# A hand-planned attention and MLP kernel: a new PE group order, load order and planner constants

## The chip, the cores and the metric

The kernel runs on one NeuronCore of a Trainium2 chip. Its time is the device time of one execution in microseconds (us); the figure that is compared is the median of several executions. A profile is one execution taken by the hardware profiler, with its own time.

The engines are named as in the profile: PE is TensorE (matmuls), PEld its weight loads, DVE is VectorE, ACT is ScalarE, POOL is GpSimd, SP is SyncE, which here does nothing but issue transfers; "SPq" is SP's queue of issues.

## What is computed

Streaming attention (four sink tokens and a window of 128) over 4 batches, 8 heads, 768 tokens and 64 dimensions, and then an MLP with the activation h * sigmoid(beta * h) on the 3072 x 512 result:

```python
keep = (pos[None, :] < 4) | ((rel >= 0) & (rel < 128))      # rel = query - key
scores = where(keep, q @ k.T / 8, -1e9);  a = softmax(scores);  x = a @ v
...
h = x @ w_in                              # 3072x512 @ 512x2048
g = h * (1.0 / (1.0 + exp(-beta * h)))
out = g @ w_out                           # 3072x2048 @ 2048x512
```

Inputs and outputs are float32; the kernel multiplies in bf16.

## The kernel before

**Tiling.** The 3072 tokens are eight halves of 384 tokens (hb 0 to 7, two to a batch). In each half there are four units, one for each pair of heads, so 32 units (u). Half 0 and half 1 (XB = 2) get their q and k transposed on PE; from half 2 on the transposes of q and k, and of the attention result, are done by the DMA engines.

**Groups.** Work on PE is cut into groups, each with a letter:

- T: q and k of one pair of heads are transposed on PE (L697) and copied to qkT (halves 0 and 1 only).
- C, D: the scores of one unit, in two parts (L783, weights of 64 rows, so that two matmuls stand side by side). Each takes a pair of PSUM banks. ACT takes the exponential (L792); POOL or DVE masks it (L798, L803, L809).
- S: the scores against the sinks (L819), with the exponential in L823. Its weights kS are made from qkT by POOL (L725).
- A: attention times v (L861, and L851 for the far blocks' sinks with vS, which DVE copies from v in L686). DVE divides by the sum (L866, L868) into onorm.
- X: the attention result is transposed on PE into xT (L880; halves 0 and 1). Later halves use a DMA transpose for it (L891).
- h, g, H: one of the 16 blocks of the first MLP product (L910, four matmuls of 384 columns), followed by tanh on ACT (L915) and the gate on DVE (L917). In halves 0 and 1 it is cut into two groups of two matmuls: h needs xT of head pairs 0 and 1, g that of 2 and 3.
- O: a quarter of a 128-token block of the second product (L931, four matmuls of 512 columns). After the fourth quarter the PSUM bank is copied to one of three buffers osb (by L558 on ACT or L563/L564 on DVE) and stored by SP (L940). The last block is cut into 384 and 128 columns.
- b: the transpose of beta (L602).

**What sets the order.** The constant ORDER is a string of 405 letters: PE does its groups in just this order. A planner, `Graph.schedule`, runs when the kernel is built. It keeps a clock for each engine, places PE's groups in the order of the string, and at each step lets each other engine take the ready operation that can start first; among those of the same start, the one with the longest tail of work behind it. Operations with several possible engines (`any_of`: casts, copies out of PSUM, masks) go where their estimated end comes first, with a small penalty for ACT (BIAS). `Graph.place` holds the planner's estimates for transfers: how long an issue takes, how many descriptors fit the ring, when a transfer lands, and what an instruction fetch costs. So the constants in it decide the order of every queue but PE's, and the choice of engines; none of them is executed on the chip. `fillers` puts matmuls on a constant tile (P<-ones, L1027) wherever the planner sees PE wait, up to 48 us by its own clock.

`resolve` then turns the plan into semaphore waits. [...]

**Loads.** All loads are issued by SP in one fixed chain. PAR['l0'] orders the eleven loads of half 0 (indices 0 to 7 are q0, k0, q1, k1, q2, k2, q3, k3, of 192 KB; 8 to 10 are v0, v1, v2, of 256 KB). PAR['mix'] interleaves the loads of half 1 and half 2 ('a') with the 16 weight pieces of 512 KB ('w'; wst and, early on, g's third buffer). Later halves follow in order, each with three blocks of q, of k and of v, in two stage buffers. SP's other work is the DMA transposes of q and k (L734), of onorm (L891) and the stores (L940).

**The lines of the loads and copies.** L635 is every load of q, k and v, L647 every weight load; L558, L560, L563 and L564 are the copies and casts on ACT, POOL and DVE, whatever tile they write.

Of the kernel before, what the change touches and what calls it, by code (L numbers as in the profile page):

```python
# [11 lines left out]
DM, DF, NOUT = 512, 2048, 512  # L12
# [7 lines left out]
EW = 256 * (NB - 1) + 128  # L20


PAR = {'MD': 1, 'XB': 2, 'l0': [0, 2, 6, 1, 3, 4, 9, 5, 7, 10, 8], 'mix': 'aawwaawawawwawwaaaawwawwawwwawaa'}
ORDER = ('TCDTSTTDCSDSCASCTADACbXXAhhhXXThghDghgDhggThgggChhgghgShDSghSghghTghgCASCAXADOXOAhhhhXOXOgOOggOOhghg'
         'hhgOOOghgghghhhghgOgOSDgSChCOghSgADODCCOODOOSAAOAOSSOCCSOSODCHHHHHHHHOHDDOHAHDCHHAHHHAAOODDOOOODCDOH'
         'SCCHHOOASSHHOHOHHHHHSHHHAACSHSOHDCCOAODDOOCCDOAOOHHSHSAOHHOHAAHHHHHHHSHOHOHOSSOCDOHDCCOHHAOOHHHHHSHH'
         'HOSOCCDOHHOHODDAHOAHAOODCCASOOOCDDHHHHHHOAOHOOSHHOOSAHHAOHHHHHOOOHHHHOOHHHHHHOOHHHHOHOOOOOHOOOOOOOOO'
         'OOOOO')


# [6 lines left out]

class Op:
    __slots__ = ("eng", "fn", "deps", "signal", "count", "waits", "sem", "vc", "dma", "seq", "end", "ns", "alts",
                 "group", "tail", "preds", "left", "succ", "at", "queue", "ring", "lag", "x", "tag", "chain")  # L40


class Group:
# [3 lines left out]
class Graph:  # L47
# [1 line left out]
    LAT = {"act": 108, "dve": 85, "gp": 45, "pe": 163, "sp": 0}  # L49
    HOP = {"act": 37, "dve": 33, "gp": 67, "pe": 57, "sp": 26}  # L50
    LAND = {"act": 22, "dve": 23, "gp": 58, "pe": 50, "sp": 26}
    LEAD, PAD, LATE = 1500, 2000, 90000
    BIAS, EARLY = 300, 100000
    FILL_TO = 48000
    RING, FETCH, SWITCH = 165, 900, 85
    DEPTH = 9

    def __init__(self):
        self.ops = []
        self.groups = []  # L60
        self.writers = {}
        self.readers = {}
        self.last_load = None
        self.filler = None

    def begin(self, tag):
# [5 lines left out]
    def add(self, eng, fn, ns=0, r=(), w=(), x=(), dma=None, alts=None, queue=470, ring=64, lag=0, after=(), tag=None):  # L72


        o = Op()
        o.eng, o.fn, o.dma, o.ns, o.alts = eng, fn, dma, ns, alts or {eng: (fn, ns)}
        o.queue, o.ring, o.lag, o.x, o.tag, o.chain = queue, ring, lag, list(x), tag, None
        o.signal, o.count, o.waits, o.vc = False, 0, [], None
        o.group, o.seq = None, -1
        if eng == "pe":  # L80
            o.group = self.groups[-1]
            o.group.ops.append(o)
        deps = []
        for k in r:
            ws = self.writers.get(k)
            assert ws, k
            deps += [(p, True) for p in ws]
        for k in w:
            deps += [(p, False) for p in self.readers.get(k, ())]
            deps += [(p, False) for p in self.writers.get(k, ())]  # L90
        for bs, i in x:
            if eng != "pe":
                deps += [(p, False) for p in bs.users[i] if p.eng == "pe"][-1:]
            bs.users[i].append(o)
            bs.left[i] += 1
        deps += [(p, False) for p in after]
        o.deps = deps
        for k in r:
            self.readers.setdefault(k, []).append(o)
        for k in w:  # L100
            self.writers[k] = [o]
            self.readers[k] = []
        self.ops.append(o)
        return o

    def place(self, o, at):
        o.at = at
        if o.dma:
            self.pending = [x for x in self.pending if x[0] > at]
            issued, need = at + o.queue + 40, min(o.ring, self.RING)  # L110
            total = sum(n for _, n in self.pending)
            for f, n in self.pending:
                if total + need <= self.RING:
                    break
                issued, total = max(issued, f), total - n
            begin = issued + o.lag if o.lag else at + 1150 + o.ns
            self.dma_free = max(self.dma_free + o.ns, begin)
            self.pending.append((self.dma_free, o.ring))
            self.free[o.eng] = issued
            o.end = self.dma_free + 950 + (self.PAD if at > self.LATE else 0)  # L120
        else:
            if o.eng == "pe":
                self.n_pe += 2
                if self.n_pe >= self.fetched + 256:
                    self.fetched += 256
                    self.dma_free = max(self.dma_free, at) + self.FETCH
                rows = o.group is not None and o.group.tag in "CD"
                if rows != self.rows:
                    at = o.at = at + self.SWITCH
                    self.rows = rows  # L130
            self.free[o.eng] = at + o.ns
            o.end = at + o.ns + self.LAT[o.eng]
# [15 lines left out]
    def schedule(self, order):  # L148
# [44 lines left out]
                t = max(t, soft[id(o)].tail + 180)  # L193
            o.tail = t + o.ns + (2000 if o.dma else 0)
        self.free = {e: 800.0 for e in self.ENGINES}
        self.dma_free, self.pending, self.n_pe, self.rows, self.fetched = 0.0, [], 0, False, 0
        new = []
        banks = [(0.0, ())] * 8
        holder = [None] * 8
# [37 lines left out]
        while at_pe < len(todo) or pool:  # L237
# [20 lines left out]
            for o in pool:  # L258
                opts = []
                for e, (fn, ns) in o.alts.items():  # L260
                    t = self.free[e]
                    for p in o.preds:
                        s = self.seen(p, e)
                        if s > t:
                            t = s
                    if o.dma:
                        t = max(t, self.dma_free - self.LEAD)
                    opts.append((t + ns + (self.BIAS if e == "act" and t < self.EARLY else 0), t, e))
                _, t, e = min(opts)
                by_eng.setdefault(e, []).append((t, o))  # L270
# [184 lines left out]
def _program(nc, G, sb, ps, q, k, v, w_in, w_out, beta, out):  # L455
# [274 lines left out]
    def XT(hb, i):  # L730
        n = "qk"[i]
        cs = list(range(NK))
        w = len(cs) * 512
        add("sp", lambda e: e.dma_start_transpose(  # L734
            qkT_all[:, hb % (NT // 4), i, cs[0] * 512:cs[0] * 512 + w].rearrange("p (b t) -> p b t", t=128),
            x16[n][hb % NX][:, cs[0]:cs[0] + len(cs), :, :].rearrange("p c h d -> p (c h d)")), 1500,
            r=[(n + "16", hb % NX, j, c_) for j in range(4) for c_ in cs],
            w=[("qkT", hb % (NT // 4), j, i, c_) for j in range(4) for c_ in cs], dma=f"dx{n}{hb % 2}", queue=1540, ring=999, lag=1350)

# [22 lines left out]
    def SC(u):  # L764
# [23 lines left out]
        for j, grp in enumerate(gs):  # L788
# [5 lines left out]
            for kind_, sg in (("d", 1), ("p", -1)):  # L794
                at_ = [i for i, blk in enumerate(grp) if blk[0] == kind_]
                if at_:
                    d = E[z][:, s0 + at_[0]:s0 + at_[-1] + 1, :, :].rearrange("p s h w -> p (s h) w")
                    alts = {"gp": (lambda e, d=d, sg=sg, at_=at_: e.affine_select(  # L798
                        d, d, [[0, 2 * len(at_)], [sg, 128]], ALU.is_ge, 0.0, base=min(sg, 0), channel_multiplier=-sg),
                        pool_ns(256 * len(at_), 2 * len(at_)))}  # L800
                    mk = maskT[:, kind_ == "p", :].unsqueeze(1).to_broadcast([128, 2 * len(at_), 128])
                    if UNITS[u][0] < PAR.get('MD', 2):
                        alts["dve"] = (lambda e, d=d, mk=mk: e.tensor_tensor(d, d, mk, ALU.mult),  # L803
                                       70 + 256 * len(at_) / 1.9)
                    any_of(alts, r=[("E", z, j), ("maskT", int(kind_ == "p"))], w=[(kind_, z, j)])
            if grp[0][0] == "s":
                d = E[z][:, s0:s0 + 2, :, :]
                mask = maskS[:, :, :].unsqueeze(2).to_broadcast([128, 2, 2, 128])
                fn = lambda e, d=d, mask=mask: e.tensor_tensor(d, d, mask, ALU.mult)  # L809
                any_of({"gp": (fn, 1150), "dve": (fn, 335)}, r=[("E", z, j), "maskS"], w=[("s", z, j)])  # L810

    def SS(u):

# [27 lines left out]
    def AV(u):  # L841
# [5 lines left out]
        for m, ps in enumerate(parts(u)):  # L847
# [8 lines left out]
            for hh in range(2):  # L856
                o0 = (2 * m + hh) * (D + 1)
                for n, (kind_, j, i, kb) in enumerate(ps):
                    vz = (hb if kb >= NK * half else hb - 1) % NV
                    add("pe", lambda e, o0=o0, hh=hh, i=i, kb=kb, vz=vz, a=(n == 0 and not far), o=(n == len(ps) - 1):  # L860
                        e.matmul(A()[:, o0:o0 + D + 1], E[z][:, i, hh, :], vaug[vz][:, kb % NK, 2 * hp + hh, :],  # L861
                                 start=a, stop=o, skip_group_check=True), 39,
                        r=[(kind_, z, j), ("v", vz, kb % NK)], x=[(bs, 0)])
        nb = c1 - c0
        av = lambda: A()[:, 0:2 * nb * (D + 1)].rearrange("p (a e) -> p a e", e=D + 1)
# [22 lines left out]
    def XO(u):  # L888
# [3 lines left out]
            xT[:, hb, hp:hp + 2, :].rearrange("p h (m t) -> p (h m) t", t=128),  # L892
            onorm[:, on:on + 2, :, :].rearrange("p o m d -> p (o m d)")), 700,
            r=[("on", on), ("on", on + 1)], w=[("xT", hp, tl), ("xT", hp + 1, tl)], dma=f"dy{on}", queue=1260,
            ring=60, lag=700)

    hi = [0]

# [26 lines left out]
    def OQ(T_, t, j, a=0, b=NOUT):  # L925
# [9 lines left out]
        if j == 3:  # L935
            z = os_i[0] % NOS
            os_i[0] += 1
            any_of(copies(osb[z][:, a:b], lambda: P[:, bk[0], a:b], {"dve": dve_ns(b - a), "act": act_ns(b - a)}, 0.5), w=[("osb", z)],
                   x=[(bk, 0)])
            add("sp", lambda e: e.dma_start(out_t[NK * hb + t][:, a:b], osb[z][:, a:b]), 640 * (b - a) // NOUT, r=[("osb", z)],  # L940
                dma=f"do{z}", queue=370, ring=8)


# [119 lines left out]
```

The softmax here doesn't subtract the row's maximum and nothing guards it: scores larger than these inputs give would overflow.

## Time and profile before

| | |
|---|---|
| median of 10 runs | 226.74 us (226.16 to 227.82) |
| the profiled execution's own time | 226.32 us |
| its span, first to last instruction | 224.6 us |
| mean granted TensorE clock | 0.992 |
| PE, first and last start of a matmul | 1.06 and 221.49 us |
| DMA traffic | 40.95 MB in 104,741 packets, mean 182 GB/s |
| L910, 512 matmuls | 92.7 us busy |
| L931, 400 matmuls issued, 379 recorded | 88.9 us busy |

A group's busy time counts the overlap of matmuls that follow each other in the pipeline once, so the mean duration of one (326 ns for an L910) is not the pace at which they go. That pace is read from the starts in the timeline or from the pieces in the chain of waits. A page's slice is a fortieth of the span, 5.6 us. In a row of the queue, start and length are those of the issue, not of the transfer.

### The profile page before, as it was taken

To read this page: it belongs to the slowest core of one execution; us is meant where nothing else is said; L and a number is where in the kernel's file an instruction comes from. 1 tells how busy PE (TensorE), PEld (TensorE's weight loads), DVE (VectorE), ACT (ScalarE), POOL (GpSimd) and SP (SyncE) were. 2 spreads that over 40 slices of the span, in tenths; PEclk is the share of its full clock that TensorE was granted. 3 is DMA by queue.
4 is the path that set the end of the run, shared out by engine and by line. 5 is a ranking of instruction groups with operands and counts; after the bars stand their busy time and mean duration, and the time that the engine had idled before them with its cause. 6 is when DMAs were issued, how large, how long until landed. Compare 5 with 4: busy or idle time off the path is not lost.

```text
span 224.6 us, 4463 instructions
## 1 busy us (share of the span) xinstructions
PE 216.1 (96%) x1699; PEld 120.0 (53%) x1720; DVE 140.2 (62%) x313; ACT 141.6 (63%) x257; POOL 66.6 (30%) x157
## 2 busy tenths in 40 slices
PE   8889999999999999999999999999999999999994
PEld 3446555555455546545554665455555556555443
DVE  1797999778757287839784569657362626455100
ACT  2595998134882867547788847678757756566221
POOL 7274345000362627352109510231436400000000
PEclk9988999999999999999999999999999999999999
DMA  7999999996999999999999999993133033101112
GB/s 159 267 344 373 354 235 329 345 236 130 220 208 220 225 192 243 179 251 221 203 243 196 200 227 236 261 240 92 47 85 82 0 85 83 47 4 47 47 47 93
DMA packets 104741, 40.95 MB, mean 182 GB/s; under 512 B 93312, under 2 KB 97680, under 8 KB 104720
## 3 DMA queue, kind: packets, MB, share of 16 engines
q1 hardware_dynamic: 103152, 40.65, 79.4%
q8 instruction: 13, 0.21, 0.4%
q10 hardware_dynamic: 1568, 0.02, 0.4%
q14 instruction: 8, 0.07, 0.1%
HBM read 27.30 MB, written 6.29 MB: 150 GB/s over the span
## 4 chain that ended last, share of the span: by engine, by line
PE 71%; DVE 9%; SPq 8%; DMA 7%; ACT 3%; issue 1%
PE P L931 31%; PE P L910 28%; SPq L635 7%; DMA v_stage<-in_v_dram 5%; PE P L861 4%; DVE g L917 4%; PE P L783 4%; DMA out_dram<-osb 2%; PE P L851 2%; ACT t L915 1%; SPq L891 1%; PE P L819 1%; PE P L1027 1%; DVE w_in L563 1%; DVE qkT L563 1%
## 5 line engine op out<-in xcount | busy, mean ns | idle before, releaser
L910 PE MATMUL P<-xT,w_in 128*128 128x384 bf16 x512 | 92.7, 326 | 0.0
L915 ACT ACTIVATE t<-P,hbeta 128x384 f32<-128x384 f32 x128 | 71.8, 586 | 31.5 <-PE P L910 25.5
L931 PE MATMUL P<-w_out,g 128*128 128x512 bf16 (+2 forms) x379 | 88.9, 370 | 1.3 <-issue 0.2
L917 DVE SCALAR_TENSOR_TENSOR g<-t,P 128x384 bf16<-128x384 f32 x128 | 68.0, 550 | 35.0 <-ACT t L915 32.3
L798 POOL TENSOR_SCALAR_AFFINE_SELECT E<-E 128x256 bf16<-128x256 bf16 (+1 forms) x109 | 52.7, 515 | 57.1 <-ACT E L792 57.1
L910 PEld LDWEIGHTS P<-xT,w_in 128*128 128x128 bf16 x512 | 48.4, 98 | 34.7 <-issue 0.8
L931 PEld LDWEIGHTS P<-w_out,g 128*128 128x128 bf16 x400 | 36.6, 98 | 36.9 <-issue 1.1
L792 ACT ACTIVATE E<-P 128x768 bf16<-128x768 f32 (+1 forms) x64 | 45.6, 760 | 15.0 <-PE P L783 14.8
L861 PE MATMUL P<-vaug,E 128*128 128x65 bf16 x352 | 19.1, 196 | 0.3 <-DVE vaug L563 0.2
L861 PEld LDWEIGHTS P<-vaug,E 128*128 128x128 bf16 x352 | 17.1, 100 | 3.6 <-ACT E L792 0.7
L558 ACT ACTIVATE osb<-P 128x512 f32<-128x512 f32 (+2 forms) x16 | 9.1, 570 | 15.2 <-PE P L931 15.1
L868 DVE TENSOR_TENSOR onorm<-P,rden 128x384 bf16<-128x384 f32 x32 | 17.5, 553 | 0.5
L783 PE MATMUL P<-qkT 64*128 64x128 bf16 (+1 forms) x256 | 16.7, 242 | 1.0 <-ACT E L792 0.4
L823 ACT ACTIVATE ES<-P 128x128 bf16<-128x128 f32 (+1 forms) x32 | 12.0, 390 | 7.0 <-PE P L819 7.0
L563 DVE CAST k<-k_stage 128x512 bf16<-128x512 f32 (+1 forms) x24 | 11.4, 473 | 6.5 <-DMA k_stage<-in_k_dram 6.4
L783 PEld LDWEIGHTS P<-qkT 64*128 64x128 bf16 x256 | 8.2, 94 | 12.4 <-issue 3.9
L851 PE MATMUL P<-vS,ES 128*128 128x130 bf16 x64 | 12.8, 223 | 0.6 <-DVE vS L686 0.4
L563 DVE CAST q<-q_stage 128x512 bf16<-128x512 f32 (+1 forms) x19 | 8.7, 455 | 7.3 <-DMA q_stage<-in_q_dram 7.1
L563 DVE CAST vaug<-v_stage 128x512 bf16<-128x512 f32 x18 | 7.9, 440 | 8.4 <-DMA v_stage<-in_v_dram 8.2
L725 POOL TENSOR_TENSOR kS<-qkT,headm 128x8 bf16<-128x8 bf16 x16 | 3.0, 209 | 32.8 <-DMA qkT<-k 29.2
L1027 PE MATMUL P<-ones 128*128 128x512 bf16 (+2 forms) x31 | 9.9, 449 | 1.1 <-POOL ones L569 1.1
L809 DVE TENSOR_TENSOR E<-E,maskS 128x512 bf16<-128x512 bf16 x16 | 8.1, 506 | 3.1 <-ACT E L792 2.9
(48 smaller groups left out, 87.9 us busy)
## 6 DMA issues: line engine op xcount, KB each, us to landing
v_stage<-in_v_dram SPq DMA_DIRECT2D x24, 256.0 KB, 4.5
out_dram<-osb SPq DMA_DIRECT2D x23, 256.0 KB, 2.5
q_stage<-in_q_dram SPq DMA_DIRECT2D x18, 256.0 KB, 4.6
k_stage<-in_k_dram SPq DMA_DIRECT2D x18, 256.0 KB, 5.8
wst<-in_moe_w_in_dram SPq DMA_DIRECT2D x5, 512.0 KB, 6.3
wst<-in_moe_w_out_dram SPq DMA_DIRECT2D x4, 512.0 KB, 7.8
g<-in_moe_w_out_dram SPq DMA_DIRECT2D x4, 512.0 KB, 7.8
q_stage<-in_q_dram SPq DMA_DIRECT2D x8, 192.0 KB, 4.6
```

The costliest lines, as they stand in the source:

```text
L563: return lambda e: e.tensor_copy(dst, at())
L635: o = add("sp", lambda e: e.dma_start(dst, src), ns, w=[("stg", n, z, j) for j in keys], dma=f"d{n}{z}{'' if i is None else i}", ring={610 ...
L783: add("pe", lambda e, dst=dst, own=own, kc=kc, rows=rows, q0=q0, nq=nq: e.matmul(dst(), tokens(own, hp, 1, rows, kc, 1)[:, 0, :], tokens(h ...
L792: add("act", lambda e, src=src, dst_=dst_: e.activation(dst_, src(), AF.Exp, bias=0.0, scale=SCALE), act_ns(256 * n), w=[(k_, z, j) for k_ ...
L798: alts = {"gp": (lambda e, d=d, sg=sg, at_=at_: e.affine_select(d, d, [[0, 2 * len(at_)], [sg, 128]], ALU.is_ge, 0.0, base=min(sg, 0), cha ...
L851: add("pe", lambda e, m=m, o0=o0: e.matmul(A()[:, o0:o0 + 2 * (D + 1)], ES[z][:, (c0 + m) * 128:(c0 + m + 1) * 128], vS[b % 2][:, 2 * hp:2 ...
L861: e.matmul(A()[:, o0:o0 + D + 1], E[z][:, i, hh, :], vaug[vz][:, kb % NK, 2 * hp + hh, :], start=a, stop=o, skip_group_check=True), 39,
L868: add("dve", lambda e: e.tensor_tensor(onorm[:, on, 2 * c0:2 * c1, :], av()[:, :, 0:D], rden[on][:, 0:2 * nb].unsqueeze(2).to_broadcast([1 ...
L910: first = add("pe", lambda e, c=c: e.matmul(hp(), w_in16[:, c, m * 128:(m + 1) * 128], xT[:, hb, c, 128 * c0:128 * c1], start=(c == 0), st ...
L915: add("act", lambda e: e.activation(tt[ti][:, 0:n], hp(), AF.Tanh, bias=0.0, scale=hbeta[:, m:m + 1]), act_ns(n) + 93, r=["hbeta"], w=[("t ...
L917: add("dve", lambda e: e.scalar_tensor_tensor(gt[hb % NG][:, m, 128 * c0:128 * c1], tt[ti][:, 0:n], 1.0, hp(), ALU.add, ALU.mult), dve_ns( ...
L931: add("pe", lambda e, m=m: e.matmul(P[:, bk[0], a:b], gt[hb % NG][:, m, t * 128:(t + 1) * 128], w_out16[:, m, a:b], start=(m == 0), stop=( ...
```

## The change

Two things are new in what the chip runs: the string ORDER and the two load orders in PAR. Beside them the planner's constants and its rules for transfers are altered: the penalty for ACT falls from 300 to 50 (and is applied only up to 10 us rather than 100), the pad on late transfers from 2.0 to 1.5 us, the ring's size from 165 to 120; instruction fetches come at a given list of PE instructions instead of every 128; some first transfers land later by a given amount; and a few estimated durations differ. An option to issue stores from ACT is added and not used (its default is SP). The instructions of the kernel, their shapes and their data are the same but for the number of fillers and the engine that does a flexible copy.

```diff
-PAR = {'MD': 1, 'XB': 2, 'l0': [0, 2, 6, 1, 3, 4, 9, 5, 7, 10, 8], 'mix': 'aawwaawawawwawwaaaawwawwawwwawaa'}
-ORDER = ('TCDTSTTDCSDSCASCTADACbXXAhhhXXThghDghgDhggThgggChhgghgShDSghSghghTghgCASCAXADOXOAhhhhXOXOgOOggOOhghg'
+PAR = {'MD': 1, 'XB': 2, 'l0': [0, 2, 6, 1, 3, 9, 4, 5, 7, 8, 10], 'mix': 'aaawwwawaawwawwaaaawwawwwwawawaa'}
+ORDER = ('TDSTTDTCCSSCCDATADSXDXAXAChbhXhTXhhgDghgggTghghghhCghgDhgShSSgTghhhggCACgADSXAXOOXAhOXhhOhOgOgggOhgOO'
...
-    LEAD, PAD, LATE = 1500, 2000, 90000
-    BIAS, EARLY = 300, 100000
+    LEAD, PAD, LATE = 1500, 1500, 90000
+    BIAS, EARLY = 50, 10000
     FILL_TO = 48000
-    RING, FETCH, SWITCH = 165, 900, 85
+    RING, FETCH, SWITCH = 120, 900, 85
     DEPTH = 9
+    FETCHES = (152, 232, 368, 477, 608, 730, 858, 988, 1111, 1222, 1354, 1482, 1601, 1728)
...
-            issued, need = at + o.queue + 40, min(o.ring, self.RING)
-            total = sum(n for _, n in self.pending)
-            for f, n in self.pending:
-                if total + need <= self.RING:
+            room = 0 if o.ring > 200 else self.RING
+            wait, total = at, sum(n for _, _, n in self.pending)
+            for b, f, n in self.pending:
+                if total <= room:
                     break
...
+            more = 450 if n in (2, 3) else 800 if o.dma == 'do0' and o.first else 0
+            if o.first and o.dma == 'dw0':
+                more = 700
+            begun = max(self.dma_free, begin - o.ns)
+            self.dma_free = max(self.dma_free + o.ns, begin) + more
...
             if o.eng == "pe":
-                self.n_pe += 2
-                if self.n_pe >= self.fetched + 256:
-                    self.fetched += 256
+                self.n_pe += 1
+                if self.n_pe in self.FETCHES:
                     self.dma_free = max(self.dma_free, at) + self.FETCH
...
-                    if o.dma:
+                    if o.dma and e == "sp":
                         t = max(t, self.dma_free - self.LEAD)
...
-            x16[n][hb % NX][:, cs[0]:cs[0] + len(cs), :, :].rearrange("p c h d -> p (c h d)")), 1500,
+            x16[n][hb % NX][:, cs[0]:cs[0] + len(cs), :, :].rearrange("p c h d -> p (c h d)")), 1250,
...
-                                       70 + 256 * len(at_) / 1.9)
+                                       150 + 256 * len(at_) / 1.6)
...
-                any_of({"gp": (fn, 1150), "dve": (fn, 335)}, r=[("E", z, j), "maskS"], w=[("s", z, j)])
+                any_of({"gp": (fn, 1150), "dve": (fn, 430)}, r=[("E", z, j), "maskS"], w=[("s", z, j)])
```

The rest of the string differs as well. The instruction lists of the two kernels, as they are built, differ on each engine: DVE has 302 instructions instead of 315, ACT 276 instead of 261, POOL 159 instead of 161, PE 1724 instead of 1722 (33 fillers instead of 31); SP has the same issues in another order.

## The prediction

> **What bounds the kernel now.** I read the page first, then the chain of waits, then the engine sums of four short windows, then the timelines of PE and of SP's queue.
>
> ```profile
> span 224.6 us, 4463 instructions
> PE 216.1 (96%) x1699; PEld 120.0 (53%) x1720; DVE 140.2 (62%) x313; ACT 141.6 (63%) x257; POOL 66.6 (30%) x157
> ...
> PE   8889999999999999999999999999999999999994
> ...
> DMA  7999999996999999999999999993133033101112
> ...
> PE 71%; DVE 9%; SPq 8%; DMA 7%; ACT 3%; issue 1%
> ...
> L1027 PE MATMUL P<-ones 128*128 128x512 bf16 (+2 forms) x31 | 9.9, 449 | 1.1 <-POOL ones L569 1.1
> ```
>
> PE is the bound: busy in every slice, 71% of the chain. The DMA engines are full too until slice 28 (about 157 us), so loads arrive just in time, and PE's lead over them is small. L1027 is no work: 31 fillers that keep PE running while it waits.
>
> Busy is not useful, so I count PE by cadence. In the chain of waits 8 L910 take 1.30 us (0.163 each) and 4 L931 take 0.86 (0.216); from the timeline's starts an L697 or L880 takes 0.056 and an L861 0.029. All useful matmuls at these rates need 194 us, against 220.4 from PE's first start (1.06) to its last (221.5). Of the other 26 us, fillers are 6.4 and about 4 are L931 records that the trace lacks (379 of 400 are there). The real loss is therefore some 16 us: 1.7 before 5 us, 6.0 from 5 to 20, 2.7 from 20 to 40, and 6 after that. These last 6 are nearly all accounted for: 23 runs of score matmuls (L783) at 0.22 each, because PE loses 0.10 before and 0.12 after each run of these 64-row tiles (start to start in the timeline, beyond the cadence), is 5.1; five waits near 63.3, 72.6, 81.9, 83.5 and 145.9 us are 1.3 more.
>
> The start, as sums of engines:
>
> ```profile
> 5.00:11.40 6.40, 5.45 (x56) 3.05 (x55) 4.98 (x10) 3.01 (x6) 1.44 (x6) 1.00 1.23 271
> 11.40:14.80 3.40, 2.42 (x32) 1.18 (x30) 2.89 (x10) 3.27 (x7) 2.85 (x8) 1.00 1.08 333
> 14.80:18.20 3.40, 3.40 (x37) 2.36 (x36) 2.94 (x10) 2.31 (x6) 2.35 (x4) 0.50 1.06 370
> 18.20:21.60 3.40, 3.40 (x41) 2.50 (x42) 3.05 (x10) 2.18 (x5) 1.21 (x3) 1.00 1.07 371
> ```
>
> Columns: window, its length, then busy time and count of PE, PEld, DVE, ACT, POOL, then granted clock, DMA share, GB/s. From 11.4 PE has little to do, from 14.8 to 18.2 its clock is 0.50, and DVE and ACT together are the pace.
>
> The middle, where the chain leaves PE:
>
> ```profile
> 65.59 3.92 DMA out_dram<-osb
> 69.51 0.02 issue
> 69.53 0.69 DVE osb L564
> ...
> 71.52 0.57 DVE onorm L868
> 72.09 0.91 SPq L891
> ```
>
> An output store stood in SP's queue behind six loads until 65.59. Its landing at 69.51 held a DVE copy into the same osb buffer; the onorm work behind it on DVE held an xT transpose at the head of SP's queue; and the v loads behind that fed the chain until 81 us, beside the waits of 72.6 and 83.5.
>
> **The change part by part.** The editable facts are the order of groups on PE, the order of loads, and which engine takes the flexible copies; the altered constants act only through these.
>
> *Load order, first half.* The v block that the sink copies (L686) need moves from eleventh load to tenth, and q2 moves one place later. In the trace those loads land at 11.18 and 12.31, so v0 is 1.1 us earlier; q2 goes from 7.54 to about 8.7. Before, PE's first L851 stood idle for 0.36 behind the copies that ended at 13.8. The qkT copies now go to ACT (0.81 each) rather than two on DVE (0.94). By hand: the first ends near 7.96 (8.21 before), T3's near 11.7 (11.89). But six exponentials then queue on ACT, the last of unit 3 ending near 17.4 against 16.95. AV of unit 0 must wait for a PSUM pair and moves from 13.14 to some 14.9. The fourth AV ends near 18.5, and the first L910 starts near 18.8 against 19.69. Behind it come X, T and the second halves (g), which wait for xT of heads 2 and 3 near 21.2; before, g began at 21.33. By then one more score group (0.22) is done. Bounds: 0.9 us gained (the first L910) to 0.9 lost (ACT carries 0.5 more by 17.4, and k11 lands 2 us later, near 19.7). I take 0.2 gained, by the g row, the nearest to steady work.
>
> *Fillers.* 31 become 33: four more before the first transposes (0.86 us at 0.216), hidden because k lands at 6.29 and its transposes start at 6.80 anyway; later ones fall from 3.6 to 2.6 us. Without that cover the longer first batch would cost its 0.86. I take 0.
>
> *Copies moved.* DVE loses 13 instructions (six osb, two qkT, four xT, two v, among exchanges), ACT gains 15. At 0.55 each that is 8 us on ACT, 141.6 to about 150 of 224.6. From 25 to 35 both are full, and DVE's list there is 0.7 shorter, ACT's the same within 0.2: 0 to 0.7 gained. I take 0, since ACT feeds DVE there; later, ACT's idle time (4.0 of 5 us from 40 to 45) hides it.
>
> *Score runs.* After the first output group they fall from 23 to 20, because C and D groups stand together more often: 3 x 0.22 = 0.65 gained. Bounds: 0 (a wait fills the room) to 3 x 0.28 = 0.84, by the widest such pair in the chain (1.03 and 0.97 for four L931 of 0.86). [...]
>
> *SP's queue.* The first output store goes ahead of the six loads of half 3, so the hold at 69.51 disappears, and two v loads instead of one stand between half 2's transposes, in a hole that the trace shows (v issued by 51.73, the k transpose at 54.42, for a DVE cast that stood behind two osb copies). ACT takes those copies now. Of the 1.3 us of waits I remove 0.5, the nearer half of 72.6 and 83.5 (0.36 + 0.53); bounds 0 and 0.9, before the losses below. What is late next is half 4's k:
>
> ```profile
> 83.78 1.08 SPq L635 DMA_DIRECT2D k_stage<-in_k_dram  x1
> 85.72 2.14 SPq L734 DMA_TRANSPOSE qkT<-q  x1
> 87.90 0.58 SPq L940 DMA_DIRECT2D out_dram<-osb  x1
> 89.55 1.45 SPq L734 DMA_TRANSPOSE qkT<-k  x1
> ```
>
> It landed at 94.00, and PE's score group started at 94.27. The change puts one v load (1.15 us of transfer) between the two transposes, and the score group 0.6 us of PE work earlier. I expect the chain cut above to repay it: SP was held 72.1 to 75.0 by xT and store, and xT's source, unit 9's AV, comes 2.5 us of PE work earlier. Half 5's scores come 3.6 earlier (from 116.89 to 113.3, k landed 115.41), with two v loads and a store fewer and one xT more before that transpose (-2.3 - 0.65 + 0.75 = -2.2): even.
>
> *Tail.* Same last output copy (0.28) and store. After the last L910 there are 17 output groups instead of 14, at the same cadence: 0.
>
> *Sum.* 0.2 + 0.65 + 0.5 = 1.35 less. The profiled execution took 226.32 (span 224.6 and 1.72 around it), so 224.97, span near 223.25. The median is 0.42 above that execution: 226.74 - 1.35 = **225.4**.
>
> **The rivals.** *Half 4's k arrives late* (slower). k lands at 94.00 + 1.15, PE sees it 0.27 later, at 95.4, where its work before is done at 93.6: a stall of 1.8, which swallows every earlier gain; of the switches 0.3 remain behind it. 226.74 + 1.8 - 0.3 = 228.2. For: the slack of 0.27 and the full DMA slices; against: the hold that goes at 69.5, and half 4's SP queue waited 1 us for a cast, in which the v's issue fits. It decides from a landing later than about 94.
>
> *The clock stays low* (about 227.3). The half clock of 14.8 to 18.2 follows a window with PE little used. If the next window, 18.2 to 21.6, is granted 0.5 as well, up to half of 3.41 is lost: 226.74 + 1.7 - 1.15. For: fillers between 8 and 18 us shrink; against: 14.8 to 18.2 holds the same AV work, and the trace let go after it. [...]
>
> *No difference.* Start and switches are filled by DMA-paced waits elsewhere; only some 0.2 remains: 226.5. For: half 2 to half 5 meet their transposes within 0.3 to 1.5 us. Against: the loss after 40 us is mostly switches, not waits. That the constants do nothing is ruled out by the instruction lists, which differ on all five engines.
>
> **How the numbers follow.** Forecast 0.50 (its own range 224.5 to 226.1), late k 0.23, low clock 0.09, no difference 0.18. A measurement here can tell about 0.3%, 0.7 us, from no change. The forecast lies all but wholly below 226.06 (0.49 of its 0.50), and 0.03 of no difference too: faster 0.52. Late k (0.22) and two thirds of the low clock (0.06) are above 227.42: slower 0.28. The rest, 0.20, is the same. Low end: 226.74 less the best bounds that go together, 0.9 + 0.65 + 0.9 = 224.3. High end: late k less a little repaid, 228.0.
>
> **What would show it.** Right: first L910 before 19.2 and g by 21.3; no DVE osb copy held by a store near 69; 20 runs of L783 after the first L931; no idle time of PE over 0.3 us before L783 near 93 and 113; span near 223.3. Wrong: a wait of L783 for qkT's k of half 4 or 5 above 1 us; a second window of clock 0.5; ACT's exponentials or tanh ending PE's or DVE's waits between 25 and 60 us by more than before; osb copies holding ACT before exponentials.

## The result, and the profile after

The changed kernel takes **229.27 us** (median of 9 executions, 228.93 to 229.88) against 226.85 for the kernel before in the same comparison (31 executions): a ratio of 1.011, 95% interval [1.0095, 1.0125]. It is slower by 2.4 us where the prediction had it faster by 1.3. On another chip, beside the last experiments, it took 230.22 against 227.19: 1.0134 [1.0114, 1.0154].

The profiled execution took 229.01 us with a span of 227.1, 2.5 longer than before. The page first, in the lines that were shown of before:

```profile
span 227.1 us, 4461 instructions
PE 216.3 (95%) x1700; PEld 119.7 (53%) x1722; DVE 134.7 (59%) x300; ACT 148.5 (65%) x272; POOL 68.8 (30%) x155
...
PE   8969998999999989999999998999999999999994
...
DMA  7999979999999899999999999993031113020012
...
PE 59%; DMA 15%; SPq 11%; ACT 7%; DVE 5%; issue 2%
...
L1043 PE MATMUL P<-ones 128*128 128x512 bf16 (+3 forms) x33 | 9.8, 435 | 1.1 <-POOL ones L583 1.1
```

PE is as busy as before (216.3 against 216.1), so the work has not grown; the span has. PE's row of slices has three 8s after its start where before there were only 9s: at 34 to 40 us, at 79 to 85 and at 136 to 142 (a slice is 5.7 us). And the chain of waits has changed its make-up: PE's part falls from 71% to 59%, that of DMA and SP's queue together grows from 15% to 26%. (Lines of code after the planner's edits stand 14 lower in the changed kernel: L924 is the old L910, L945 the old L931, L797 the old L783, L931 the old gate L917. The stores, L956, and the fillers, L1043, stand 16 lower.)

The start, as sums of engines in the same four windows:

```profile
5.00:11.40 6.40, 6.40 (x58) 3.50 (x58) 3.79 (x10) 3.37 (x6) 1.27 (x4) 1.00 1.23 271
11.40:14.80 3.40, 1.68 (x19) 0.64 (x18) 3.10 (x9) 3.40 (x7) 1.91 (x5) 1.00 1.06 307
14.80:18.20 3.40, 3.33 (x40) 2.56 (x42) 2.95 (x7) 3.09 (x9) 3.10 (x5) 0.57 1.02 359
18.20:21.60 3.40, 3.40 (x50) 2.29 (x47) 3.36 (x10) 2.89 (x5) 2.41 (x5) 0.93 1.08 378
```

Nothing is won or lost here: the first L924 starts at 19.82 where the first L910 started at 19.69, and by 40 us PE has lost, in waits, switches and fillers, 16.95 us against 16.8. So the 2.4 us come later. The chain of waits of the changed kernel, from 71 us (start, length, what):

```profile
71.15 0.57 DVE onorm L882
71.72 0.31 SPq L748
...
72.08 0.88 SPq L956
...
73.01 1.26 SPq L905
...
74.32 0.58 SPq L649
...
74.94 5.28 DMA v_stage<-in_v_dram
...
80.24 0.43 DVE vaug L577
80.67 0.94 DVE g L931 x2
```

Read downwards: the transpose of k (L748) is at the head of SP's queue; its issue began at 70.51, and the view follows it back to an onorm on DVE, a tile that it doesn't read. Behind it stand a store and an xT transpose (issued at 72.08 and 73.01), and behind these the v loads of half 3, which are issued from 74.3 on and land at 79.2, 80.2 and 81.2. That is nearly the old picture (the old v landed at 78.5, 80.9 and 82.0: the first is 0.7 us later now, the others 0.7 and 0.8 earlier). DVE's timeline of the changed kernel (in brackets: idle before, and what ended it):

```profile
71.15 0.56 DVE L882 TENSOR_TENSOR onorm<-P,rden 128x384 bf16<-128x384 f32 x1
79.21 0.43 DVE L577 CAST vaug<-v_stage 128x512 bf16<-128x512 f32 x1 [7.50 <-DMA v_stage<-in_v_dram]
79.56 0.55 DVE L931 SCALAR_TENSOR_TENSOR g<-t,P 128x384 bf16<-128x384 f32 x1
80.24 0.43 DVE L577 CAST vaug<-v_stage 128x512 bf16<-128x512 f32 x1
80.58 2.87 DVE L931 SCALAR_TENSOR_TENSOR g<-t,P 128x384 bf16<-128x384 f32 x6
```

DVE stands for 7.50 us at the cast of a v block that hasn't landed, with seven gates behind it in its list, none of which goes before it. The kernel before had this cast at the head of DVE's list too, with gates behind it:

```profile
76.98 0.69 DVE L564 TENSOR_SCALAR osb<-P 128x512 f32<-128x512 f32 x1 [1.89 <-DMA out_dram<-osb]
78.55 0.43 DVE L563 CAST vaug<-v_stage 128x512 bf16<-128x512 f32 x1 [0.88 <-DMA v_stage<-in_v_dram]
78.90 1.01 DVE L917 SCALAR_TENSOR_TENSOR g<-t,P 128x384 bf16<-128x384 f32 x2
```

What is new is when the gates are due. The first tanh of these products starts at 77.64 there and at 76.91 here, the first gate at 78.90 there and only at 79.56 here. PE meanwhile goes on with products and then waits twice for a gate (0.30 us at 80.16, 0.21 at 81.19). PE's timeline of the changed kernel shows that, and one wait more in front of it, for the xT itself:

```profile
75.19 0.50 PE L924 MATMUL P<-xT,w_in 128*128 128x384 bf16 x2
76.11 3.75 PE L924 MATMUL P<-xT,w_in 128*128 128x384 bf16 x22 [0.42 <-DMA xT<-onorm]
80.16 0.82 PE L924 MATMUL P<-xT,w_in 128*128 128x384 bf16 x4 [0.30 <-DVE g L931]
81.19 0.34 PE L833 MATMUL P<-qkT,kS 128*128 128x384 bf16 x1 [0.21 <-DVE g L931]
```

In the kernel before the same products of half 2 began at 76.30 and went through 32 of them without a wait:

```profile
76.30 5.37 PE L910 MATMUL P<-xT,w_in 128*128 128x384 bf16 x32
```

The second xT of that half landed at 75.93 there and at 76.07 here. The data come 0.14 us later, the products are asked for 1.1 us earlier. Two more places where PE gets there ahead of the data, from PE's and DVE's timelines of the changed kernel. At half 4's scores it waits for the transposed k itself, at half 6's for gates that stand behind casts of half 7's q:

```profile
95.08 0.56 PE L797 MATMUL P<-qkT 64*128 64x128 bf16 x12 [0.33 <-DMA qkT<-k]
...
141.72 0.45 PE L797 MATMUL P<-qkT 64*128 64x128 bf16 x8 [0.77 <-DVE g L931]
142.52 1.04 PE L945 MATMUL P<-w_out,g 128*128 128x512 bf16 x4 [0.35 <-DVE g L931]
```
```profile
139.05 0.43 DVE L577 CAST q<-q_stage 128x512 bf16<-128x512 f32 x1 [1.65 <-DMA q_stage<-in_q_dram]
139.39 1.01 DVE L931 SCALAR_TENSOR_TENSOR g<-t,P 128x384 bf16<-128x384 f32 x2
```

Counted start to start beyond the cadence and the switches to score groups (0.22 us each, read from the kernel before), PE's waits after 60 us are:

| near | us | ended by |
|---|---|---|
| 75.4 | 0.6 | xT of half 2 lands |
| 79.5 to 81.7 | 1.1 | gates behind a v cast on DVE |
| 94.4 | 0.4 | k of half 4 lands |
| 98.3 to 98.9 | 0.35 | exponentials on ACT |
| 140.7 to 142.5 | 1.25 | gates behind q casts on DVE |

Together 3.7 us against 1.0 before. The prediction had 1.3 before, in five waits; two of these, near 63.3 and 145.9, are places where the trace holds three of the four records of an L931 group (a row with x3), so the gap of 0.2 us there is a missing record and no wait.

### The profile page after: what moved, and what is told of

It is laid out like the page before. It is cut to its first block, busy times and chain, and to the rows that moved or that the text cites. A ratio compares the mean times of both kernels' runs of the same rounds, so it can differ in the third digit from the quotient of the medians.

```text
span 227.1 us, 4461 instructions
## 1 busy us (share of the span) xinstructions
PE 216.3 (95%) x1700; PEld 119.7 (53%) x1722; DVE 134.7 (59%) x300; ACT 148.5 (65%) x272; POOL 68.8 (30%) x155
## 4 chain that ended last, share of the span: by engine, by line
PE 59%; DMA 15%; SPq 11%; ACT 7%; DVE 5%; issue 2%
PE P L945 28%; PE P L924 23%; SPq L649 7%; DMA q_stage<-in_q_dram 6%; DMA v_stage<-in_v_dram 6%; DVE g L931 3%; PE P L875 3%; PE P L797 3%; ACT E L806 3%; ACT t L929 2%; DMA k_stage<-in_k_dram 2%; SPq L905 1%; SPq L956 1%; PE P L865 1%; SPq L661 1%
## 5 line engine op out<-in xcount | busy, mean ns | idle before, releaser
L924 PE MATMUL P<-xT,w_in 128*128 128x384 bf16 x512 | 95.0, 326 | 1.0 <-DMA xT<-onorm 0.4
L945 PE MATMUL P<-w_out,g 128*128 128x512 bf16 (+2 forms) x378 | 88.8, 370 | 1.8 <-issue 0.5
L931 DVE SCALAR_TENSOR_TENSOR g<-t,P 128x384 bf16<-128x384 f32 x128 | 67.8, 549 | 35.6 <-ACT t L929 32.7
L812 POOL TENSOR_SCALAR_AFFINE_SELECT E<-E 128x256 bf16<-128x256 bf16 (+1 forms) x107 | 53.8, 532 | 76.2 <-ACT E L806 76.1
L924 PEld LDWEIGHTS P<-xT,w_in 128*128 128x128 bf16 x512 | 47.2, 98 | 36.6 <-DVE g L931 2.0
L945 PEld LDWEIGHTS P<-w_out,g 128*128 128x128 bf16 x400 | 36.9, 98 | 37.0 <-issue 0.9
L572 ACT ACTIVATE osb<-P 128x512 f32<-128x512 f32 (+2 forms) x22 | 12.7, 578 | 20.6 <-PE P L945 17.6
L797 PE MATMUL P<-qkT 64*128 64x128 bf16 (+1 forms) x256 | 16.9, 242 | 2.4 <-ACT E L806 0.9
L577 DVE CAST vaug<-v_stage 128x512 bf16<-128x512 f32 x16 | 7.1, 445 | 17.6 <-DMA v_stage<-in_v_dram 17.3
L797 PEld LDWEIGHTS P<-qkT 64*128 64x128 bf16 x256 | 8.2, 94 | 13.6 <-issue 3.7
L577 DVE CAST q<-q_stage 128x512 bf16<-128x512 f32 (+1 forms) x19 | 9.5, 498 | 7.8 <-DMA q_stage<-in_q_dram 7.8
L577 DVE CAST k<-k_stage 128x512 bf16<-128x512 f32 (+1 forms) x24 | 11.4, 473 | 3.9 <-DMA k_stage<-in_k_dram 3.6
L823 DVE TENSOR_TENSOR E<-E,maskS 128x512 bf16<-128x512 bf16 x16 | 7.6, 478 | 6.3 <-ACT E L806 6.2
L1043 PE MATMUL P<-ones 128*128 128x512 bf16 (+3 forms) x33 | 9.8, 435 | 1.1 <-POOL ones L583 1.1
```

Of the source, the lines that this page charges most:

```text
L577: return lambda e: e.tensor_copy(dst, at())
L797: add("pe", lambda e, dst=dst, own=own, kc=kc, rows=rows, q0=q0, nq=nq: e.matmul(dst(), tokens(own, hp, 1, rows, kc, 1)[:, 0, :], tokens(h ...
L924: first = add("pe", lambda e, c=c: e.matmul(hp(), w_in16[:, c, m * 128:(m + 1) * 128], xT[:, hb, c, 128 * c0:128 * c1], start=(c == 0), st ...
L931: add("dve", lambda e: e.scalar_tensor_tensor(gt[hb % NG][:, m, 128 * c0:128 * c1], tt[ti][:, 0:n], 1.0, hp(), ALU.add, ALU.mult), dve_ns( ...
L945: add("pe", lambda e, m=m: e.matmul(P[:, bk[0], a:b], gt[hb % NG][:, m, t * 128:(t + 1) * 128], w_out16[:, m, a:b], start=(m == 0), stop=( ...
```

## The experiments

Twelve kernels, in three lots, each compared with the kernel before on its own chip. The first lot asks which part of the change carries the loss, the second whether single holds do, the third whether it is the data's pace or the order itself.

**1. New string and loads, old planner.**

```diff
-PAR, ORDER = (before)      # in the kernel before
+PAR, ORDER = (changed)
```

> The new ORDER and load orders, scheduled by the old planner (its constants and transfer rules). Theory 'early landings' (the altered constants let loads land too soon in the plan, so casts stand at the head of DVE's queue in front of gates): the loss goes, 226.5 to 227.3 us, and DVE's 7.5 us wait for v_stage near 72 to 79 is gone or holds no g. Rival 'group order' (the new string itself asks PE for late data): 228.8 to 229.6, with the waits near 75, 94 and 141 still there. Rival 'mismatch' (a string searched for one planner is bad with any other): above 230.

Measured 232.57 us, ratio 1.0251 [1.0212, 1.0289]. The longest wait of PE, from its timeline:

```profile
120.10 1.15 PE L910 MATMUL P<-xT,w_in 128*128 128x384 bf16 x6 [2.18 <-DVE g L917]
```

**2. Old string and loads, new planner** (the same exchange in the changed kernel).

> The old ORDER and load orders, scheduled by the new planner. 'Early landings': about 229, with DVE waiting several us for a v load in front of g. 'Group order': 226.5 to 227.2. 'Mismatch': above 230.

Measured 231.85, ratio 1.022 [1.0173, 1.0267]; PE's longest wait is 1.20 us at 121.3, for an exponential on ACT.

**3. Only the two load orders.**

```diff
-'l0': [0, 2, 6, 1, 3, 4, 9, 5, 7, 10, 8], 'mix': 'aawwaawawawwawwaaaawwawwawwwawaa'
+'l0': [0, 2, 6, 1, 3, 9, 4, 5, 7, 8, 10], 'mix': 'aaawwwawaawwawwaaaawwawwwwawawaa'
```

> The old kernel with only the two load orders of the new one (l0 and mix). Both theories put the loss behind 60 us, so 226.3 to 227.5; a first L851 without the wait for vS. If the load order alone costs, 228 or more, and both theories lack a part.

Measured 231.62, ratio 1.0199 [1.0155, 1.0243], far above 226.3 to 227.5: by this expectation's own words both theories lack a part. PE waits 1.86 us for an xT:

```profile
80.85 0.82 PE L910 MATMUL P<-xT,w_in 128*128 128x384 bf16 x4 [1.86 <-DMA xT<-onorm]
```

**4. Landings taken as later from 48 us.** The changed kernel, with the planner's pad of 1.5 us applied from 48 us on instead of 90.

```diff
-    LEAD, PAD, LATE = 1500, 1500, 90000
+    LEAD, PAD, LATE = 1500, 1500, 48000
```

> The new kernel with one number changed: the planner's pad of 1.5 us on landings applies from 48 us instead of 90 us. 'Early landings': casts of half 3 move behind gates, so the waits of 1.1 us near 80 go: 227.7 to 228.4 (those near 141 stay). 'Group order': 229.0 to 229.6.

Measured 232.79, ratio 1.0248 [1.0207, 1.0289], outside both expectations, with a wait of 3.30 us for an xT:

```profile
79.94 0.82 PE L924 MATMUL P<-xT,w_in 128*128 128x384 bf16 x2 [3.30 <-DMA xT<-onorm]
```

What follows from these four: each is 2.0 to 2.5% slower than the kernel before, and slower than the changed kernel too (1.1 and 1.3%). In all four the planner plans anew, and each new plan has a wait of 1 to 3 us in another place, also where the constants are the more careful ones (4). Runs 1 and 2 lie above 230, where the expectations had string and plan that fit only each other; no run tests that reading by itself. So the size of a part can't be had by putting it in alone; whether string or constants carry the loss stays open after them. The next lot therefore leaves string and plan as they are and moves single operations afterwards.

**5 to 8. Single casts moved back in their queue.** In the changed kernel, after planning, an operation is put behind the next k of its engine's list, never behind one that needs its result:

```diff
     G.schedule(ORDER)
+    G.defer(("cast", 3, "v", 1), 6)      # 5: half 3's v casts, behind the gates
+    G.defer(("cast", 3, "v", 0), 6)
+    G.defer(("cast", 7, "k", 0), 2)      # 6: half 7's casts
+    G.defer(("cast", 7, "q", 2), 2)
+    G.defer(("cast", 7, "q", 1), 2)
+    G.defer(("cast", 7, "q", 0), 4)
+    G.defer(("load", 4, "v", 0), 1)      # 8: half 4's first v load behind the transpose of k
...
+    def defer(self, what, k):
+        x = self.named[what]
+        ops = self.ops
+        at = ops.index(x)
+        users = {id(o) for o in ops if any(p is x for p, _ in o.deps)}
+        to, left = at, k
+        for i in range(at + 1, len(ops)):
+            if id(ops[i]) in users or left == 0:
+                break
+            if ops[i].eng == x.eng:
+                to, left = i, left - 1
+        ops.insert(to, ops.pop(at))
+        for i, o in enumerate(ops):
+            o.seq = i
```

5, half 3's v casts alone:

> The new kernel with its plan kept, but two casts of half 3's v on DVE moved behind six gates (g); nothing is planned again. 'Head of queue' (a cast that waits for a late load at the head of DVE's queue delays gates that were ready, and PE waits for those): the PE waits of 0.46 + 0.37 + 0.30 us near 80 go, time down by 0.9 to 1.2 us, to about 228.2. 'DMA pace' (PE would wait for the same data a little later anyway): the waits move to the scores or AV behind, time within 0.3 us of 229.3.

Measured 230.60, ratio 1.0145 [1.012, 1.017]: no gain, and outside both expectations. The gates did leave the cast's shadow, four in a row on DVE with only ACT's tanh ahead of them; but PE had waited before that already (DVE's timeline, then PE's):

```profile
79.11 2.09 DVE L949 SCALAR_TENSOR_TENSOR g<-t,P 128x384 bf16<-128x384 f32 x4 [6.79 <-ACT t L947]
```
```profile
77.48 2.77 PE L942 MATMUL P<-xT,w_in 128*128 128x384 bf16 x16 [1.19 <-DMA xT<-onorm]
```

The xT that landed at 76.07 in the changed kernel landed at 77.44 here, and the wait of 0.42 became 1.19; half 4's scores then waited 0.7. The moved casts are not the cause of that: they stand behind it. This execution was late from a q load on that was issued at 31.9 and landed at 39.6 (37.5 to 38.4 in the other kernels that share the plan), and SP's queue was 0.8 us behind at 59.5. In run 7, with the same move, the xT landed at 75.73, and 28 products went without a wait:

```profile
75.51 4.72 PE L946 MATMUL P<-xT,w_in 128*128 128x384 bf16 x28
```

So the move removes the wait for the gates at this place; what it is worth in time is read from 7 against 6. Why the six executions of run 5 are all above 230 stays open.

6, half 7's casts alone:

> The same for half 7: its q casts on ACT and DVE and its first k cast move behind two to four tanh or gate operations. 'Head of queue': the waits of 0.84 and 0.42 us near 141 go, time down by 0.9 to 1.3 us, to about 228.1. 'DMA pace': no change, or the transposes of half 7 come late.

Measured 229.08, ratio 1.0072 [1.0044, 1.01]: by the ratios 0.9 us less than the changed kernel's first measurement, as 'Head of queue' had it. PE's timeline near 142 has its 0.77 and 0.35 no more:

```profile
141.21 0.81 PE L944 MATMUL P<-xT,w_in 128*128 128x384 bf16 x4
141.96 0.56 PE L817 MATMUL P<-qkT 64*128 64x128 bf16 x12
142.59 1.04 PE L965 MATMUL P<-w_out,g 128*128 128x512 bf16 x4
```

This hold was a cause of its own; it stands near the end of the full stretch of the DMA engines, and no later wait took its place.

7, both:

> Both moves together. 'Head of queue': the two add, 2.0 to 2.4 us less, 226.9 to 227.3, the time of the kernel before. 'DMA pace': 229.0 or more.

Measured 228.46, ratio 1.0062 [1.0036, 1.0089], 227.30 to 230.14 over 12 executions. By the ratios some 1.1 of the 2.4 us came back, between the two expectations. Against run 6, which lacks only half 3's move, it is 0.6 us less, and the intervals overlap: half 3's share is not shown to have come back. Two longer waits stand in the trace now, 1.16 at 84.0 and 1.45 at 93.9; the second from DVE's timeline:

```profile
94.37 0.22 DVE L722 COPY vS<-vaug 4x260 bf16<-4x260 bf16 x1 [1.81 <-ACT vaug L594]
94.51 0.54 DVE L904 TENSOR_TENSOR onorm<-P,rden 128x384 bf16<-128x384 f32 x1
94.98 0.53 DVE L953 SCALAR_TENSOR_TENSOR g<-t,P 128x384 bf16<-128x384 f32 x1
```

Again an operation on late data (the sink copy vS, which needs the v block that ACT casts when it lands) at the head of DVE's list, with a gate behind it.

8, both and half 4's first v load behind the transpose of k, which was the one between the two transposes that the prediction had named:

> Both moves, and on SP's queue half 4's k transpose goes ahead of the v load that stands before it. The wait of 0.40 us near 94 for qkT should go: 0.2 to 0.4 us below the run with both moves. If the v cast on ACT, which then waits for a later landing, holds the exponentials behind it, no gain or a loss up to 1 us.

Measured 231.43, ratio 1.0192 [1.0159, 1.0225]: the loss that its expectation had as its bad case, and larger. The v block lands at 94.96 instead of 93.68, and the same vS copy now stands 3.71 us, PE 3.32:

```profile
96.85 0.39 PE L968 MATMUL P<-w_out,g 128*128 128x512 bf16 x1 [3.32 <-DVE g L954]
```

So v stood rightly ahead of k: moved back by one place, this load costs 3.0 us against run 7.

**9 to 12. Is it the data's pace, or the order itself?** One lot on one chip: the changed kernel again; the kernel before and the changed kernel with half of the bytes of q, k and v from half 3 on; and the casts of half 4 moved as well.

```diff
             dst, keys, ns = stg[n][z][:, i, :, :], [i], 1150
+            if hb >= 3:
+                src, dst = src[:, 0:4, :], dst[:, 0:4, :]
```

(for v, and in the same way for q and k; the plan's own estimate stays at 1150, so each queue's order is unchanged).

> The changed kernel once more, on the same chip as the three kernels beside it. Every theory expects 1.011 of the kernel before (1.008 to 1.014); on the record stand 1.0110 for it, 1.0072 with half 7's casts behind the gates and 1.0062 with half 3's too. If it comes out at 1.006 to 1.008 here, those two have gained nothing.

> The kernel before, with the loads of q, k and v of halves 3 to 7 cut to heads 0 to 3 (the other heads keep what the buffers held), so 45 loads of 256 KB carry 128 KB; plan, string and instructions stay. At the pace of the trace (182 GB/s on the mean, more in the full stretch) that takes some 28 us of traffic out. Both theories expect little of the kernel before: its waits of DMA or DVE after 60 us are 1.3 us, of which 0.5 to 1.0 goes: ratio 0.994 to 0.999.

> The changed kernel with the same cut. Theory 'work asked for ahead of its data': the new string and plan put casts, scores and products before the landings of a DMA stream that keeps its pace, so with the data early nearly all of the 4.1 us of waits after 60 us goes (0.5 to 1.0 stays), and the 0.65 of the score runs is left as a gain: 225.3 to 226.5 against some 226 for the old kernel with this cut, so the new minus the old with the cut lies between -0.9 and +0.4 us. Rival 'the new order is worse in itself' (exponentials, gates and casts in a worse order on ACT and DVE, whatever the data do): the new one stays 1.5 us or more behind the old one with the same cut.

| kernel | us | ratio to the kernel before (227.19) |
|---|---|---|
| changed, again | 230.22 | 1.0134 [1.0114, 1.0154] |
| before, half loads | 225.35 | 0.9913 [0.9895, 0.9932] |
| changed, half loads | 225.52 | 0.9932 [0.9912, 0.9953] |

The changed kernel again shows the waits of the table: 1.25 and 0.5 near 80, 0.4 at 95, 0.35 at 99, 1.25 near 142; only the one for the xT of half 2, which landed at 75.92, is missing. The cut gives the kernel before 1.84 us and the changed kernel 4.70. The 1.84 is more than was expected (ratio 0.9913 against 0.994 to 0.999) and more than all waits counted in the kernel before; what else it gained is not shown. What the changed kernel gets beyond the other, 2.86, is what it had lost (3.03). So the order is not worse in itself. With the data early the two are level: 0.17 us apart, with overlapping intervals, inside the expected -0.9 to +0.4 and far from the rival's 1.5. (The cut takes bytes from the whole stream, and other transfers move too: in the kernel before, a DVE copy into osb that waits for a store goes at 73.57 with half loads and at 74.40 without. Which landing counts most it does not tell.) The chains of waits of the two, the old kernel first:

```profile
PE 83%; DVE 7%; DMA 3%; ACT 3%; SPq 2%; issue 1%
```
```profile
PE 86%; ACT 9%; DVE 2%; issue 1%; POOL 0%; POOLq 0%
```

In the new one DMA and SP's queue, 26% and 17% in the two profiles of the changed kernel as it is, are not in the chain any more. The same products of half 2, and the v cast on DVE, from the timelines of the changed kernel with half loads:

```profile
75.86 4.72 PE L928 MATMUL P<-xT,w_in 128*128 128x384 bf16 x28
```
```profile
77.18 0.46 DVE L577 CAST vaug<-v_stage 128x512 bf16<-128x512 f32 x1 [4.80 <-DMA v_stage<-in_v_dram]
77.86 0.56 DVE L935 SCALAR_TENSOR_TENSOR g<-t,P 128x384 bf16<-128x384 f32 x1 [0.22 <-ACT t L933]
```

28 products without a wait, in the same order as the one that stalled. DVE still stands 4.80 us at the cast, but the v block lands before the gates are due (the first waits 0.22 for its tanh), and that idle time costs nothing. None of the waits in the table above is left; what PE still loses after 70 us are, but for missing records, the switches to score groups.

The last one, half 4 as well (on DVE the cast of q's block 1 and the two vS copies, on ACT the cast of v's block 0):

```diff
+    G.defer(("cast", 4, "q", 1), 2)
+    G.defer(("cast", 4, "v", 0), 1)
+    G.defer(("vS", 4, 1), 1)
+    G.defer(("vS", 4, 0), 3)
```

> The changed kernel with half 3's v casts and half 7's casts behind gates as before (1.0062), and now half 4 as well: on DVE the cast of q's block 1 behind two gates and the sink copies vS behind one, two and three operations that are ready, on ACT the cast of v's block 0 behind one tanh. No wait is taken away and no cast is missing; only the order on the two queues changes. Theory 'a late landing at the head of an in-order queue': the two waits that were left, 1.16 at 84.0 and 1.45 at 93.9, fall to 0.8 or less together, and the ratio to 0.996 to 1.002. Rival 'the landings set the pace and the wait only moves to the next group that needs them': 1.004 to 1.009, with a new wait over 0.7 between 85 and 100.

Measured 228.66, ratio 1.0067 [1.0043, 1.0091], no better than 1.0062. Both of the old waits on gates are gone; PE's timeline shows others, for the transposed k itself at 94.8 and for a POOL copy (made from such a k) at 132.8, and 0.65 at 75.7 for an xT:

```profile
94.80 0.56 PE L823 MATMUL P<-qkT 64*128 64x128 bf16 x12 [0.67 <-DMA qkT<-k]
...
132.77 0.23 PE L859 MATMUL P<-qkT,kS 128*128 128x128 bf16 x1 [0.61 <-POOL kS L765]
```

Here the rival's numbers came: 1.0067 lies in its 1.004 to 1.009, and PE waits 0.7 for the k at 94.8. In this run the wait moved to the next group that needed a landing. No version that I ran with all of its loads beats the kernel before.

## Why the prediction was wrong

**The step that failed is the term for SP's queue**, the 0.5 us gained, with the sentence that half 4's k and half 5's scores would be repaid by "the chain cut above". I had priced the loads that become earlier and taken the earlier demand as covered. The cut is there: the copy out of PSUM that a store held at 69.5 on DVE is on ACT, and unit 9 comes earlier. (That copy waits 2.42 us for a store at 71.16 there; the next work on ACT, at 73.67, waits for PE, so that costs nothing.) But the DMA engines stay full to about 152 us, through slice 27 of the page, not to 157 as the prediction read it (a share of 1.15 from 147 to 152 and 0.48 from 152 to 157; 1.11 and 0.28 before), and the landings follow the bytes: half 3's first v takes 4.9 us from issue (74.3) to landing (79.2), and 2.7 with half of the bytes, where its cast goes at 77.18 and not at 79.21. So half 2's k landed at 57.70 (58.15 before), half 3's v at 79.19 (78.53), half 4's k at 95.04 (94.00), half 5's k at 114.02 (115.41), half 7's last q at 139.88 (141.95): some 0.5 to 2 us to either side. Where PE waits, the string asks earlier by more than the data gain: the products of half 2 by 1.1 us, while the v on which their gates hang comes 0.7 later; the scores of half 6 by 2.8, while the q in front of their gates comes 1 to 2 earlier. In place of 0.5 gained stand 2.7 us of added waits. That these are waits for data, and not a worse order, runs 10 and 11 show.

**Half 4's k**, the slower rival: the landing was right (95.15 worked out, 95.04 measured, 5.8 us from issue where it had been 4.4), the price not (1.8 worked out, 0.4 measured). PE got there at 94.7 and not at 93.6, late by the waits of 75 to 82. So these waits didn't add up: the 1.1 us by which PE came later shortened the wait for the k. In run 12 two waits went and others came, with the time the same (1.0067 against 1.0062 in run 7).

**Copies moved, "I take 0".** I looked at how full ACT would be, and that held: 148.5 us busy (some 150 forecast). I didn't look at what stands at the head of each list when the gates behind it are due earlier. Sixteen v casts on DVE wait 17.3 us for landings, where eighteen waited 8.2 before. That is how a late load reaches PE although PE has no business with that load until 85 us, six later. Half 7's share, the 1.25 us near 141, was recovered by moving four casts (1.0110 and 1.0134 without, 1.0072 with, on different chips, each against the kernel before on its own); half 3's was not.

**Score runs, 0.65 gained.** Twenty runs after the first output group instead of 23: as read. That it is worth 0.65 is not shown: with half loads, where hardly a wait is left in either, the medians are level within 0.17.

**Start, 0.2 gained.** It came out at 0.1 to 0.2 lost; the first L924 at 19.82 lies outside what was to be seen (19.2). ACT is busy through the whole window before it (3.40 of 3.40 from 11.4 to 14.8), which is the load that I had as the bound on the losing side; that ACT is the cause wasn't tried.

**Fillers and tail, 0.** Right: the fillers are busy for 9.8 us (9.9 before), and the span ends 3.1 us after the last start of a matmul in both. **The clock** (the second rival): no second low window. The low stretch is 3.41 us at 0.50 in both profiles (14.79 to 18.21 before, 15.25 to 18.66 after), with 1.00 behind it. What sets it no run shows, and little use of PE ahead of it is not enough: in the changed kernel with half loads PE is busy for 2.43 of 3.40 us from 11.4 to 14.8 (2.42 before), and the clock is 1.00 from 5 to 21.6. More on it below.

The ledger: 226.74, +0.15 start, -0.65 score runs, +2.7 waits, gives 228.9 of 229.27; with nothing for the score runs it gives 229.6. The 0.3 to either side I can't place, so the ledger doesn't tell whether the shorter score runs paid.

What stays open: whether the string or the planner's constants ask too early (runs 1 to 4 can't separate them), and whether a string exists that keeps 20 score runs and the old margins.

## What to carry over

Where the DMA engines are full, read an order against the landings: for each group list when its last operand lands and when PE gets there, and count each microsecond of earlier demand beyond the old margin as a wait unless the load itself moves earlier. For each load look also at the operation that stands first behind it on DVE, ACT and POOL, and at what waits in line behind that one. To learn whether a slower order is bad in itself or only ahead of its data, cut the bytes of the loads and leave everything else, in both kernels: here that took two runs, where four exchanges of parts couldn't tell.

## What I had not expected of the hardware

- The half clock near 15 to 18 us comes and goes between executions. In the changed kernel's profile the granted clock is 0.57 from 14.8 to 18.2 and 0.93 from 18.2 to 21.6: the 3.41 us at 0.50 again, some 0.5 us later than before. In the profile of the changed kernel with half loads, whose instructions and loads are the same up to 57 us, it is 1.00 in all four windows. Four executions of the changed kernel on one chip took 230.11, 230.44, 230.19 and 230.25 us at mean clocks of 0.992, 0.993, 1.000 and 0.993. In these executions the low window has no price that can be told from the scatter.
- Landing times shift between executions of the same instructions. The xT transpose of half 2 landed at 76.07 and at 75.92 in two profiles of the changed kernel, and between 75.73 and 77.44 in five others whose instructions are planned alike up to there. The kernel before asks for it 0.37 us after its landing (75.93, 76.30), a margin well inside this spread.
